# Last 64 query rows of two heads: laid side by side by GpSimd and turned in one transpose

## The chip, the cores and the metric

One core of one Trainium2 chip runs the program. The metric is the time of one execution on the device in microseconds (us), median of several runs. An engine of the core works through its own instructions in order: PE (TensorE matmul; its weight loads are shown apart as PEld), DVE (VectorE), ACT (ScalarE), POOL (GpSimd) and SP (SyncE, which here only issues transfers). Engines wait for each other through semaphores.

## The reference, cut to what matters

Three blocks follow each other on 4 batches of 576 rows by 512 columns: attention with 8 heads of 64 columns, then two feed-forward blocks. The change is in the attention alone.

```python
scores = scale * np.matmul(q, k.transpose(0, 1, 3, 2)) + bias
attn = np.exp(scores - np.max(scores, axis=-1, keepdims=True))
attn = attn / (np.sum(attn, axis=-1, keepdims=True) + 1e-09)
x = np.matmul(attn, v)
x = x.transpose(0, 2, 1, 3).reshape(B, S, H * D)
x = x + relu(layernorm(x) @ w_ch1) @ w_ch2
```

The third block takes x in the same way, with a gate across the rows.

## The kernel before, in words

A first stage (up to some 53 us) works out the bias from the positions, writes it to DRAM and reads it back as tiles. The attention (some 53 to 325 us) follows, then the two feed-forward blocks (to 954 us), where the weights arrive as 64-bit numbers and are converted on DVE, ACT and POOL.

**The attention** goes through 16 units, one for a pair of heads and a batch (`UNITS`). In a unit the 576 query rows of both heads make nine tiles of 128 rows, numbered 0 to 8: four of each head, and tile 4, which holds the last 64 rows of both heads. For a tile PE makes the scores (`S`, line 687), DVE adds the bias and finds the row maximum (`add`, L693), ACT takes the exponent (`exp`, L707), PE turns the result (`T`, L713 and `RT`, L721 and L723), ACT and DVE split it into a high and a low part (`hi`, `lo`). Products with f32 operands are made of such parts, for precision: K, Q and V are split too, by POOL, in `split_k` (L238), `split_q` and `split_v` with the pairs L113 (copy to the high part) and L119 (the rest). `split_k` makes `kh` and `kl` of head 0, then of head 1.

**The outputs.** `PV` (L776) multiplies V with the turned weights, so a head's output comes out turned: 128 partitions (V's high part's 64 columns, then its low part's 64) by 576 rows. `Pev` (L779, ACT) copies each half of 288 rows to the tile `psb` of the head. For the four full tiles `O` (L782) turns 128 columns of `psb` into `OB`; `Oev` copies that to SBUF, `fo` (POOL, L792) adds the two halves of 64, `fx` (POOL, L804) multiplies by the reciprocal of the sum and stores through SP. For the last 64 rows of both heads `Or` (L812) does turning and adding in one: a product of the 64 columns of `psb` with the constant `fold`, two unit matrices of 64 on top of each other. `xr` (DVE, L817) multiplies by the reciprocal and issues two stores from SP.

```python
for h in range(2):
    pe.matmul(PB[64 * h:64 * h + 64, 288:288 + D], lhsT=Psb[h][:, place(4)], rhs=fold, start=True, stop=True)
```

The columns that `place(4)` names are 256 to 319, which lie in both halves of 288, so they are there for both heads after the last of a unit's four `Pev`, called `Pev 1 1`.

**What sets the order.** The table `SEQ` (L27) is the order in which a unit's steps are written out: an entry names a unit relative to the one at hand (`-1` the last one, whose outputs are finished here, `1` the next), a step and its arguments. No scheduler moves anything; each engine gets its instructions in this order. The program of unit u so holds `Pev 1 1`, `Or`, `xr`, `fo`, `fx` of unit u-1, the splits of K and V for unit u+1 (`kh`, `vh`) and of Q for u+2 (`sq`), and the first scores of u+1 (`1 S 0`). At the head of a step `slot` transfers are issued by SP: `slot 0` moves the split Q of the next unit to its place (`place_q`, L236), `slot 5` loads Q and K for u+2 (L210, L216), `vh` loads V. `1 S 0` needs the Q that `place_q` moved and `kh`, `kl` of head 0. The table `END` (L50) is the same for what is left of the last unit, mixed with the layer norms (`N`, `P`), and products (`H`) of the first feed-forward block. In the last units POOL also has the scale of the layer norms (L469 to L473), the applying of some (L479) and splits of the first weights (`w1l`, `w2l`) in its order.

Of the kernel before, what the change touches and what calls it, by code (L numbers as in the profile page):

```python
# [9 lines left out]
F32 = mybir.dt.float32  # L10
# [3 lines left out]
AF = mybir.ActivationFunctionType  # L14
ALU = mybir.AluOpType
# [3 lines left out]
B, H, S, D, DM = 4, 8, 576, 64, 512  # L19
# [8 lines left out]
    0 slot 0, 0 T 0, -1 O 0 1, 0 exp 2, -1 RThi 8 1, -1 lo 8, 0 hi 0, 0 add 3, 0 slot 1, 0 T 1, 0 C 0, -1 RTlo 6 0, 0 add 4, -1 PV 1 0 0 5, -1 RTlo 8 1,  # L28
    0 exp 3, 0 lo 0, 0 S 5, 0 C 1, 0 hi 1, 0 RT 1 0, 0 RThi 1 0, 0 exp 4, -1 O 0 3, 0 lo 1, -1 O 0 2, -1 PV 1 0 5 10, 0 slot 2, 0 T 2, 0 S 6, 0 RTlo 1 0,
    0 add 5, -1 Pev 1 0, 0 hi 2, -1 O 0 0, -1 ra, 0 RT 4 0, 0 slot 3, 0 T 3, -1 PV 1 1 0 1, -1 PV 1 1 1 10, 0 RThi 4 0, 0 lo 2, -1 Oev 0, 0 hi 3, 0 exp 5,  # L30
    0 add 6, 0 RTlo 4 0, 0 kh, -1 Pev 1 1, 0 slot 4, 0 T 4, 0 S 7, 0 hi 4, -1 rb, 0 exp 6, 0 lo 3, 0 S 8, 0 add 7, 0 lo 4, -1 O 1 0, 0 RT 3 1,
    -1 Or, 0 RThi 3 1, -1 O 1 3, -1 O 1 2, 0 PV 0 0 0 2, -1 xr, 0 slot 5, 0 T 5, 0 vh, 0 exp 7, 0 RTlo 3 1, 0 hi 5, 1 S 0, 0 cp, -1 O 1 1, -1 fo 0,
    -1 Oev 1, -1 fo 1, 0 add 8, -1 fx, 0 sq, 0 slot 6, 0 T 6, 0 PV 0 0 2 10, 1 add 0, 0 lo 5, 0 hi 6, 0 exp 8, 0 RT 6 0, 1 S 1, 1 S 2, 0 slot 7, 0 T 7,
    0 RT 8 1, 0 lo 6, 0 Pev 0 0, 1 exp 0, 1 add 1, 0 slot 8, 0 T 8, 0 hi 7, 0 PV 0 1 0 10, 0 RThi 6 0, 0 hi 8, 1 S 3, 1 add 2, 1 S 4, 1 exp 1, 0 Pev 0 1,
# [13 lines left out]
AP_AT = [(15, 0), (15, 1), (15, 4), (15, 5)]  # L48

END = [w.strip() for w in """  # L50
    O 0 1, RThi 8 1, lo 8, RTlo 6 0, PV 1 0 0 5, RTlo 8 1, N 0, N 1, O 0 3, O 0 2, PV 1 0 5 10, Pev 1 0, O 0 0, ra, PV 1 1 0 1, PV 1 1 1 10, N 2, N 3, Oev 0, F 3, Pev 1 1, rb, fo 0, O 1 0, O 1 3, O 1 2, O 1 1, P 0, P 1, H 0 0 6, Or, Oev 1, fo 1, xr, fx, P 2, H 0 6 12, P 3, H 1 0 12
""".split(",")]
WARM = 8
AHEAD = 2
# [45 lines left out]
def block_kernel(  # L100
# [6 lines left out]
    act, dve, pool, pe, sp = nc.scalar, nc.vector, nc.gpsimd, nc.tensor, nc.sync  # L107
# [32 lines left out]
    const = new_pool("const", 1)  # L140
    psT = new_pool("psT", 1, space=PSUM)
    PT = [psT.tile([128, 4, 128], F32, name=f"pt{z}") for z in range(2)]
    ident = const.tile([128, 128], F32, name="ident")
    fold = const.tile([128, 64], F32, name="fold")
    mhalf = const.tile([128, 1], F32, name="mhalf")
    gains = const.tile([128, 8], F32, name="gains")

# [133 lines left out]
    with ExitStack() as c:  # L281
        p = new_pool("bk", 1, c)
# [20 lines left out]
        for f in (load_q, load_k):  # L303
# [9 lines left out]
            out=W.rearrange("p (g h) -> p g h", h=8), in0=w8.unsqueeze(1).to_broadcast([128, 4, 8]), in1=ind.unsqueeze(2).to_broadcast([128, 4, 8]), op=ALU.mult,  # L313
# [98 lines left out]
        for y, z in enumerate(ORDER):  # L412
            mark(f"bias {y}")
            m += [units(n) for n in ORDER[y + AHEAD:][:1]]
            if y in FILL:
                busy(1)
            late.append((z, sums(z, m[y])))
            if y >= BEHIND:
                finish(*late.pop(0))
            if y == WARM_EXP:  # L420
                act.activation(w8[:, :1], mhalf, AF.Exp)
            if y == 5:
                load_v(0, raw0)
# [218 lines left out]
    with ExitStack() as c:  # L642
        smp = new_pool("asm", 1, c)
        sm = smp.tile([128, 48], F32, name="sm")
        SU, RC = [sm[:, 9 * z:9 * z + 9] for z in range(2)], [sm[:, 18 + 9 * z:27 + 9 * z] for z in range(2)]
# [6 lines left out]
        RT = [[atp.tile([128, 2, 320], F32R, name=f"rt{z}{w}") for w in "hl"] for z in range(2)]  # L652
# [3 lines left out]
            dve.memset(t[64:, :, :32].bitcast(F32), 0.0)  # L656
        AT = [tuple(atp.tile([128, 4, S], F32R, name=f"at{h}{w}") for w in "hl") for h in range(2)]
        pp = new_pool("ap", 1, c)
        Psb = [pp.tile([128, S], F32, name=f"psb{h}") for h in range(2)]
        Ob = pp.tile([128, 2, 4, 128], F32, name="ob")  # L660
        xp = new_pool("ax", 1, c)
        M["rc"] = c.enter_context(ExitStack())
        psP = new_pool("psP", 1, c, space=PSUM, side="right")
        PB = psP.tile([128, 512], F32, name="PB")
        OB = psP.tile([128, 512], F32, name="OB")
# [96 lines left out]
        def pv_bank(u, h, x):  # L762
            return SB[0][:, 0] if (u, h, x) == (NU - 1, 1, 1) else PB
# [12 lines left out]
                pe.matmul(d, lhsT=w, rhs=m, start=q == 0, stop=q == len(terms) - 1)  # L776

        def emit_Pev(u, h, x):
            act.activation(Psb[h][:, 288 * x:288 * x + 288], pv_bank(u, h, x)[:, :288], AF.Copy)  # L779

        def emit_O(u, h, t):
            pe.transpose(OB[:, 128 * t:128 * t + 128], Psb[h][:, place(t)], ident)  # L782

        xt = {}

# [22 lines left out]
                M["loads", u]()  # L808

        def emit_Or(u):  # L810
            for h in range(2):
                pe.matmul(PB[64 * h:64 * h + 64, 288:288 + D], lhsT=Psb[h][:, place(4)], rhs=fold, start=True, stop=True)  # L812

        def emit_xr(u):
            hp, b = UNITS[u]
            xr = xp.tile([128, D], F32, name="xr")
            dve.tensor_scalar(out=xr, in0=PB[:, 288:288 + D], scalar1=RC[u % 2][:, 4:5], scalar2=None, op0=ALU.mult)  # L817
            for h in range(2):
                (act if u == NU - 1 else sp).dma_start(out=xs[b][512:, 128 * hp + D * h:128 * hp + D * h + D], in_=xr[64 * h:64 * h + 64])

# [22 lines left out]
        def emit_slot(u, n):  # L843
# [479 lines left out]
def host_arrays(inputs):  # L1323
    q, k, v = (np.asarray(inputs[n]) for n in ("q", "k", "v"))
    d = {}
    qt = q.transpose(0, 1, 3, 2).reshape(B, 4, 2, D, S)
    q2 = np.empty((B, 4, 2, D, S), q.dtype)
    q2[:, :, 0] = qt[:, :, 0]
    q2[:, :, 1, :, :64] = qt[:, :, 1, :, 512:]
    q2[:, :, 1, :, 64:] = qt[:, :, 1, :, :512]  # L1330
    d["q"] = q2.reshape(B, 4, 128, S)
    kt = k.transpose(0, 1, 3, 2).reshape(B, 4, 2, D, S).transpose(0, 1, 3, 2, 4)[:, :, None]
    k2 = np.empty((B, 4, 2, D, 2, S + 64), k.dtype)
    k2[..., :64] = kt[..., 512:]
# [36 lines left out]
    d["moe2_w_sg"] = np.ascontiguousarray(w.transpose(1, 0, 2)).reshape(128, 5 * S)
    return d
# [24 lines left out]
```

## Time and profile before

| | |
|---|---|
| median of 3 runs | 955.36 us (955.33 to 957.57) |
| the profiled execution, its own time | 955.95 us |
| its span, first to last instruction | 954.0 us |
| busy: PE / PEld | 930.1 / 806.4 us |
| busy: DVE / ACT / POOL | 723.2 / 498.2 / 418.5 us |
| granted clock of TensorE, mean | 1.00 (the level of 2.4 GHz) |

A row of the timeline has the start of an instruction, how long it took, the engine, the line, the operation, what it writes and reads, and how many equal ones follow each other. A bracket at the end says how long the engine stood idle before it and what ended that. Where the engine named there had long been done, it was another, often a transfer. Matmuls are pipelined and their ends are modelled, so starts are the better guide on PE and PEld. The first unit's K is split at some 51 us, and a unit takes 16.4 to 17.2 us from then on.

### The profile page before, as it was taken

What the parts mean: (1) busy time and instruction counts of PE and PEld (TensorE: products, weight loads), DVE (VectorE), ACT (ScalarE), POOL (GpSimd) and SP (SyncE); (2) the same over time, 40 slices, a digit from 0 to 9 for tenths busy, and PEclk for the clock granted to TensorE, in tenths of its full rate; (3) what the DMA queues carried; (4) which work ended last, traced back from release to release, by engine and by line L of the source; (5) the groups of instructions that cost most, each with busy time, mean ns of one, the idle gap of its engine ahead of it and who ended that gap; (6) DMA issues with size and microseconds to landing.
All of it is one profiled execution on the core that took longest, in us unless ns stands there. A gap on an engine that the chain in (4) does not pass through costs nothing. (4 is left out here: it accounts for less than half of the span.)

```text
span 954.0 us, 16102 instructions
## 1 busy us (share of the span) xinstructions
PE 930.1 (97%) x5729; PEld 806.4 (85%) x5729; DVE 723.2 (76%) x1441; ACT 498.2 (52%) x1108; POOL 418.5 (44%) x523
## 2 busy tenths in 40 slices
PE   7889999999999999999999999999999999999997
PEld 2269999999999778888888888888788998989996
DVE  7988999999889587886679797979755656455452
ACT  8979999999998654221222222322132635253340
POOL 0057787878888634332223343334300523143241
PEclk9999999999999999999999999999999999999999
DMA  6878766748643451103032323332321100001001
GB/s 237 278 232 258 217 186 197 224 133 265 193 140 109 158 189 45 67 21 110 21 98 98 119 90 122 98 110 84 120 71 67 59 1 12 34 1 56 1 35 66
DMA packets 58127, 110.26 MB, mean 116 GB/s; under 512 B 10176, under 2 KB 21184, under 8 KB 57792
## 3 DMA queue, kind: packets, MB, share of 16 engines
q1 hardware_dynamic: 56960, 108.38, 35.5%
q8 instruction: 45, 0.74, 0.3%
q10 hardware_dynamic: 1088, 0.87, 0.3%
q14 instruction: 34, 0.28, 0.1%
HBM read 71.41 MB, written 28.38 MB: 105 GB/s over the span
## 5 line engine op out<-in xcount | busy, mean ns | idle before, releaser
L123 PE MATMUL psh<-blk,w1h 128*128 128x512 f32 (+1 forms) x640 | 151.5, 368 | 1.1 <-DVE blk L119 1.0
L176 POOL TENSOR_TENSOR cvl<-cvl,cvt 128x512 f32<-128x512 f32 x44 | 56.9, 1293 | 207.8 <-DVE cvt L173 188.3
L638 ACT ACTIVATE hh<-psh 128x512 fp32r<-128x512 f32 (+1 forms) x80 | 43.8, 553 | 179.3 <-PE psh L123 179.1
L123 PEld LDWEIGHTS psh<-blk,w1h 128*128 128x128 f32 x640 | 113.3, 188 | 22.2 <-PE OB L782 1.2
L693 DVE CUSTOM_DVE_ANT_0 ct<-s,bias 128x576 f32<-128x576 f32 x144 | 107.1, 752 | 17.5 <-PE s L687 9.8
L707 ACT ACTIVATE a<-ct,sm 128x576 f32<-128x576 f32 x144 | 112.1, 779 | 3.5 <-DVE sm L693 2.9
L1043 DVE TENSOR_TENSOR x_sb<-psy,x_sb 128x512 f32<-128x512 f32 x144 | 97.3, 683 | 9.1 <-PE psy L123 8.6
L639 DVE SCALAR_TENSOR_TENSOR hl<-psh,hh 128x512 fp32r<-128x512 f32 (+1 forms) x80 | 50.5, 633 | 56.2 <-ACT hh L638 56.2
L123 PE MATMUL psy<-w2h,hh 128*128 128x512 f32 x288 | 90.9, 396 | 1.3 <-ACT hh L638 0.7
L123 PE MATMUL psy<-w2l,hh 128*128 128x512 f32 x288 | 88.9, 390 | 0.0
L123 PE MATMUL psy<-w2h,hl 128*128 128x512 f32 x288 | 88.8, 390 | 0.0
L713 PE MATMUL pt<-ident,a 128*128 128x128 f32 x576 | 85.1, 273 | 0.7 <-DVE at0l L119 0.7
L123 PE MATMUL psh<-blk,w1l 128*128 128x512 f32 (+1 forms) x320 | 79.0, 368 | 0.0
L687 PE MATMUL s<-kh,q 128*128 128x288 f32 x320 | 72.0, 314 | 3.2 <-DVE sm L693 1.8
L713 PEld LDWEIGHTS pt<-ident,a 128*128 128x128 f32 x576 | 68.6, 140 | 2.0 <-DVE at0l L119 1.4
L687 PE MATMUL s<-kl,q 128*128 128x288 f32 x320 | 65.9, 295 | 0.0
L123 PEld LDWEIGHTS psh<-blk,w1l 128*128 128x128 f32 x320 | 56.8, 188 | 10.0
L123 PEld LDWEIGHTS psy<-w2h,hl 128*128 128x128 f32 x288 | 54.1, 188 | 11.5
L123 PEld LDWEIGHTS psy<-w2l,hh 128*128 128x128 f32 x288 | 54.0, 188 | 11.4
L123 PEld LDWEIGHTS psy<-w2h,hh 128*128 128x128 f32 x288 | 52.3, 188 | 12.8 <-DVE x_sb L1043 2.0
L177 POOL TENSOR_TENSOR cvw<-cvl,cvw 128x512 f32<-128x512 f32 x44 | 60.0, 1364 | 3.5
L687 PEld LDWEIGHTS s<-kh,q 128*128 128x128 f32 x320 | 48.9, 189 | 5.8 <-DVE sm L693 2.7
(191 smaller groups left out, 2171.5 us busy)
## 6 DMA issues: line engine op xcount, KB each, us to landing
r<-in_moe_w_ch_dram SPq DMA_DIRECT2D x32, 512.0 KB, 4.9
k<-in_k_dram SPq DMA_DIRECT2D x16, 640.0 KB, 4.7
q<-q SPq DMA_DIRECT2D x64, 144.0 KB, 3.9
scr<-o SPq DMA_DIRECT2D x24, 295.5 KB, 3.2
v<-in_v_dram SPq DMA_DIRECT2D x16, 384.0 KB, 5.5
q<-in_q_dram SPq DMA_DIRECT2D x16, 288.0 KB, 3.0
bias<-scr SPq DMA_DIRECT2D x8, 576.0 KB, 5.9
bias<-scr SPq DMA_DIRECT2D x8, 512.0 KB, 6.5
```

What stands on the lines that cost most here:

```text
L123: pe.matmul(ps, lhsT=w, rhs=x, start=start and j == 0, stop=stop and j == len(terms) - 1)
L176: pool.tensor_tensor(out=T["l"], in0=T["l"], in1=T["t"].bitcast(F32), op=ALU.mult)
L177: pool.tensor_tensor(out=T["w"], in0=T["l"], in1=T["w"], op=ALU.add)
L638: act.activation(hh[:, f, :n], ps[:, :n], AF.Relu)
L639: dve.scalar_tensor_tensor(out=hl[:, f, :n], in0=ps[:, :n], scalar=0.0, in1=hh[:, f, :n].bitcast(F32), op0=ALU.max, op1=ALU.subtract)
L687: pe.matmul(s[:, x, :288], lhsT=w, rhs=m[:, 288 * x:288 * x + 288], start=j == 0, stop=j == len(prs) - 1)
L693: dve.tensor_tensor_reduce(out=ct, in0=s[:, :, :288], in1=bias[UNITS[u][0]][:, n].rearrange("p (a b) -> p a b", a=2), scale=-0.125, scalar ...
L707: act.activation(weights(n), ct.rearrange("p a b -> p (a b)"), AF.Exp, scale=-1.0, bias=mt, accum_out=SU[u % 2][:, n:n + 1])
L713: pe.transpose(PA[k % 2][:, j], e[:, 128 * j:128 * j + 128], ident)
L1043: dve.tensor_tensor(out=x_sb[:, t], in0=ps, in1=x_sb[:, t], op=ALU.add)
```

## The change

`Psb` becomes one tile for both heads. A new step `oc` has POOL copy the last 64 rows of both heads side by side into the new tile `Pr` (128 by 2 by 64). `Or` turns `Pr` in one transpose against the unit matrix instead of two products with `fold`, which goes with its load. `xr` scales 128 columns instead of 64 on DVE, and POOL adds the two halves of 64 before the two stores. In `SEQ` the step `Pev 1 1` with `oc` behind it now stands ahead of `kh`, where `kh` stood first; in `END` `oc` stands behind `Pev 1 1`.

```diff
-    0 add 6, 0 RTlo 4 0, 0 kh, -1 Pev 1 1, 0 slot 4, 0 T 4, ...
+    0 add 6, 0 RTlo 4 0, -1 Pev 1 1, -1 oc, 0 kh, 0 slot 4, 0 T 4, ...
...
-    ... Oev 0, F 3, Pev 1 1, rb, fo 0, ...
+    ... Oev 0, F 3, Pev 1 1, oc, rb, fo 0, ...
...
-        Psb = [pp.tile([128, S], F32, name=f"psb{h}") for h in range(2)]
+        Psb = pp.tile([128, 2, S], F32, name="psb")
+
+        Pr = pp.tile([128, 2, 64], F32, name="pr")
...
         def emit_Or(u):
-            for h in range(2):
-                pe.matmul(PB[64 * h:64 * h + 64, 288:288 + D], lhsT=Psb[h][:, place(4)], rhs=fold, start=True, stop=True)
+            pe.transpose(PB[:, 288:416], Pr.rearrange("p h c -> p (h c)"), ident)
+
+        def emit_oc(u):
+            pool_copy(Pr, Psb[:, :, place(4)])
...
+            w = xp.tile([128, 2 * D], F32, name="xw")
             xr = xp.tile([128, D], F32, name="xr")
-            dve.tensor_scalar(out=xr, in0=PB[:, 288:288 + D], scalar1=RC[u % 2][:, 4:5], scalar2=None, op0=ALU.mult)
+            dve.tensor_scalar(out=w, in0=PB[:, 288:416], scalar1=RC[u % 2][:, 4:5], scalar2=None, op0=ALU.mult)
+            pool.tensor_tensor(out=xr, in0=w[:, :D], in1=w[:, D:], op=ALU.add)
```

How this moves instructions is read from the order of the two programs (line numbers of the changed one are one or two lower). First POOL's order in one unit, before: `sm` is a step for the reciprocal, `kh` and `kl` are K's splits for the next unit, `v` those of V, `x<-ob` the step `fo`.

```order
L795 TENSOR_SCALAR sm<-sm 128x9 [waits Activation_49]
L113 TENSOR_SCALAR kh<-k 128x640 [waits DMAHW5_49,PE_49]
L119 TENSOR_TENSOR kl<-k,kh 128x640 [waits PE_49,Pool_49]
L113 TENSOR_SCALAR kh<-k 128x640
L119 TENSOR_TENSOR kl<-k,kh 128x640 [waits Pool_49]
L113 TENSOR_SCALAR v_103<-v 128x12x64 [waits DMAHW6_49,PE_49]
L119 TENSOR_TENSOR v_103<-v,v_103 128x12x64 [waits Pool_49]
L792 TENSOR_TENSOR x<-ob 128x4x64 [waits DMAHW0_49,Activation_49]
```

The same piece of the changed program:

```order
L794 TENSOR_SCALAR sm<-sm 128x9 [waits Activation_49]
L113 TENSOR_SCALAR pr<-psb 128x128 [waits Activation_49]
L113 TENSOR_SCALAR kh<-k 128x640 [waits DMAHW4_49]
L119 TENSOR_TENSOR kl<-k,kh 128x640 [waits Pool_49]
L113 TENSOR_SCALAR kh<-k 128x640
L119 TENSOR_TENSOR kl<-k,kh 128x640 [waits Pool_49]
L820 TENSOR_TENSOR xr<-xw 128x64 [waits DMAHW2_49,DMAHW1_49,DVE_49]
L113 TENSOR_SCALAR v_102<-v 128x12x64 [waits DMAHW5_49,PE_49]
L119 TENSOR_TENSOR v_102<-v,v_102 128x12x64 [waits Pool_49]
L791 TENSOR_TENSOR x<-ob 128x4x64 [waits DMAHW7_49]
```

The copy, which waits for `Pev 1 1` on ACT, now stands ahead of both heads' `kh` and `kl`, and the addition `xr<-xw` ahead of V's split.

On PE the steps from `Or` to `1 S 0` stood so before (`s<-kh` and `s<-kl` in the last rows are the next unit's first scores):

```order
L782 MATMUL OB<-ident,psb_891 128x128 [waits Activation_49]
L723 MATMUL s_905<-ident,a_866 128x128
L812 MATMUL PB<-fold,psb_890 64x64 [waits Activation_49]
L812 MATMUL PB<-fold,psb_891 64x64
L782 MATMUL OB<-ident,psb_891 128x128 x2
L776 MATMUL PB<-at0h,v_104 128x288 [waits Activation_49,Pool_49]
L776 MATMUL PB<-at0h,v_104 128x288
L713 MATMUL pt_73<-ident,a_865 128x128 [waits DVE_49]
L713 MATMUL pt_73<-ident,a_865 128x128 x3
L687 MATMUL s_901<-kh,q_101 128x288 [waits DMAHW2_49,DMAHW3_49,DVE_49,Pool_49]
L687 MATMUL s_901<-kh,q_101 128x288
L687 MATMUL s_901<-kl,q_101 128x288 [waits Pool_49]
```

And now:

```order
L781 MATMUL OB<-ident,psb 128x128 [waits Activation_49]
L722 MATMUL s_903<-ident,a_864 128x128
L810 MATMUL PB<-ident,pr 128x128 [waits Pool_49]
L781 MATMUL OB<-ident,psb 128x128 x2
L775 MATMUL PB<-at0h,v_103 128x288 [waits Activation_49]
L775 MATMUL PB<-at0h,v_103 128x288
L712 MATMUL pt_73<-ident,a_863 128x128 [waits DVE_49]
L712 MATMUL pt_73<-ident,a_863 128x128 x3
L686 MATMUL s_899<-kh,q_100 128x288 [waits DMAHW1_49,DMAHW2_49,DVE_49,Pool_49]
L686 MATMUL s_899<-kh,q_100 128x288
L686 MATMUL s_899<-kl,q_100 128x288 [waits Pool_49]
```

One transpose stands where two products stood and waits for POOL instead of ACT; the order on PE is the same otherwise. The wait of `s<-kl` for POOL was there before; it is for `kl` of head 0.

The last piece is POOL's in the last unit's program, of the changed kernel (`t<-t,rs` applies a layer norm, `w2l` is a weight's low part, `pr` the copy):

```order
L476 TENSOR_SCALAR t<-t,rs 128x512 [waits DMAHW4_49]
L794 TENSOR_SCALAR sm<-sm 128x9 [waits Activation_49]
L563 TENSOR_SCALAR gains<-gains 128x4
L119 TENSOR_TENSOR w2l<-t,w2h 128x512
L113 TENSOR_SCALAR pr<-psb 128x128 [waits Activation_49]
L119 TENSOR_TENSOR w2l<-t,w2h 128x512
L820 TENSOR_TENSOR xr<-xw 128x64 [waits DMAHW4_49,DMAHW3_49,DVE_49]
```

Before, nothing of `Or` hung on this order; now the copy comes behind the first `w2l`.

## Rows read from the trace of the kernel before

**Rows 1.** The page's first part: busy us (share of the span) xinstructions.

```profile
PE 930.1 (97%) x5729; PEld 806.4 (85%) x5729; DVE 723.2 (76%) x1441; ACT 498.2 (52%) x1108; POOL 418.5 (44%) x523
```

**Rows 2.** Windows: us, PE, PEld, DVE, ACT, POOL busy, clock, DMA share, GB/s.

```profile
62.00:67.00 5.00, 3.12 (x22) 2.48 (x22) 3.73 (x12) 3.52 (x11) 2.61 (x2) 1.00 1.00 321
...
255.00:272.00 17.00, 17.00 (x140) 16.77 (x140) 14.10 (x39) 15.52 (x42) 13.25 (x16) 1.00 0.71 224
```

**Rows 3.** Timeline of PEld (weight loads) in unit 12's program: start, us, what.

```profile
262.70 0.14 PEld L782 LDWEIGHTS OB<-ident,psb 128*128 128x128 f32 x1
262.83 0.14 PEld L723 LDWEIGHTS s<-ident,a 128*128 128x128 f32 x1
...
263.40 0.20 PEld L782 LDWEIGHTS OB<-ident,psb 128*128 128x128 f32 x2
...
264.53 0.33 PEld L687 LDWEIGHTS s<-kl,q 128*128 128x128 f32 x2
```

**Rows 4.** Timeline of ACT: the step Pev 1 1 in units 9, 12, 13 and 14.

```profile
212.95 0.41 ACT L779 ACTIVATE psb<-PB 128x288 f32<-128x288 f32 x1
...
261.83 0.40 ACT L779 ACTIVATE psb<-PB 128x288 f32<-128x288 f32 x1
...
278.21 0.40 ACT L779 ACTIVATE psb<-PB 128x288 f32<-128x288 f32 x1
...
294.58 0.40 ACT L779 ACTIVATE psb<-PB 128x288 f32<-128x288 f32 x1
```

**Rows 5.** Timeline of PEld: 1 S 0 in unit 9.

```profile
215.41 0.33 PEld L687 LDWEIGHTS s<-kl,q 128*128 128x128 f32 x2
```

**Rows 6.** Timeline of POOL in units 12 to 15.

```profile
255.69 0.73 POOL L113 TENSOR_SCALAR kh<-k 128x640 fp32r<-128x640 f32 x1
256.50 1.58 POOL L119 TENSOR_TENSOR kl<-k,kh 128x640 fp32r<-128x640 f32 x1
...
261.59 0.83 POOL L113 TENSOR_SCALAR v<-v 128x768 fp32r<-128x768 f32 x1 [1.16 <-PE PB L776]
...
273.46 0.73 POOL L113 TENSOR_SCALAR kh<-k 128x640 fp32r<-128x640 f32 x1
...
283.05 1.20 POOL L804 TENSOR_TENSOR x<-x,sm 128x256 f32<-128x256 f32 x2
...
289.53 0.73 POOL L113 TENSOR_SCALAR kh<-k 128x640 fp32r<-128x640 f32 x1
...
310.96 2.53 POOL L119 TENSOR_TENSOR w2l<-t,w2h 128x512 fp32r<-128x512 f32 x2
```

**Rows 7.** Groups of POOL by form: xcount | busy us, mean ns of one | idle before.

```profile
L119 POOL TENSOR_TENSOR grl<-sq,grh 128x64 fp32r<-128x64 f32 x16 | 5.2, 327 | 0.0
L113 POOL TENSOR_SCALAR x2h<-rh 128x256 fp32r<-128x256 f32 x4 | 1.6, 410 | 33.8 <-ACT rh L116 33.8
L113 POOL TENSOR_SCALAR w<-m 128x1 f32<-128x1 f32 x1 | 0.2, 192 | 45.5 <-DVE m L335 45.5
```

**Rows 8.** Timeline of SP: loads for the layer norms, then place_q for unit 15.

```profile
288.89 1.75 SPq L610 DMA_DIRECT2D t<-xs  x4
290.75 2.41 SPq L236 DMA_DIRECT2D q<-q  x4
```

**Rows 9.** Timeline of PEld: 1 S 0 of unit 15, and Or in unit 15's program.

```profile
297.26 0.30 PEld L687 LDWEIGHTS s<-kh,q 128*128 128x128 f32 x2 [0.20 <-POOL v L119]
...
313.11 0.20 PEld L812 LDWEIGHTS PB<-fold,psb 128*64 128x64 f32 x4 [0.17 <-issue]
```

**Rows 10.** The tile q: issue to landing of its transfers.

```profile
DMA to landing us min/median/max: 2.4/3.5/7.8
```

**Rows 11.** Timeline of POOL and of PE at the end of the attention.

```profile
329.09 1.43 POOL L792 TENSOR_TENSOR x<-ob 128x256 f32<-128x256 f32 x2
...
328.09 0.34 PE L812 MATMUL PB<-fold,psb 128*64 128x64 f32 x4
```

More of the change, by code (lines that the diff above doesn't have):

```diff
@@ L30 @@
     0 add 5, -1 Pev 1 0, 0 hi 2, -1 O 0 0, -1 ra, 0 RT 4 0, 0 slot 3, 0 T 3, -1 PV 1 1 0 1, -1 PV 1 1 1 10, 0 RThi 4 0, 0 lo 2, -1 Oev 0, 0 hi 3, 0 exp 5,
-    0 add 6, 0 RTlo 4 0, 0 kh, -1 Pev 1 1, 0 slot 4, 0 T 4, 0 S 7, 0 hi 4, -1 rb, 0 exp 6, 0 lo 3, 0 S 8, 0 add 7, 0 lo 4, -1 O 1 0, 0 RT 3 1,
+    0 add 6, 0 RTlo 4 0, -1 Pev 1 1, -1 oc, 0 kh, 0 slot 4, 0 T 4, 0 S 7, 0 hi 4, -1 rb, 0 exp 6, 0 lo 3, 0 S 8, 0 add 7, 0 lo 4, -1 O 1 0, 0 RT 3 1,
     -1 Or, 0 RThi 3 1, -1 O 1 3, -1 O 1 2, 0 PV 0 0 0 2, -1 xr, 0 slot 5, 0 T 5, 0 vh, 0 exp 7, 0 RTlo 3 1, 0 hi 5, 1 S 0, 0 cp, -1 O 1 1, -1 fo 0,
@@ L50 @@
 END = [w.strip() for w in """
-    O 0 1, RThi 8 1, lo 8, RTlo 6 0, PV 1 0 0 5, RTlo 8 1, N 0, N 1, O 0 3, O 0 2, PV 1 0 5 10, Pev 1 0, O 0 0, ra, PV 1 1 0 1, PV 1 1 1 10, N 2, N 3, Oev 0, F 3, Pev 1 1, rb, fo 0, O 1 0, O 1 3, O 1 2, O 1 1, P 0, P 1, H 0 0 6, Or, Oev 1, fo 1, xr, fx, P 2, H 0 6 12, P 3, H 1 0 12
+    O 0 1, RThi 8 1, lo 8, RTlo 6 0, PV 1 0 0 5, RTlo 8 1, N 0, N 1, O 0 3, O 0 2, PV 1 0 5 10, Pev 1 0, O 0 0, ra, PV 1 1 0 1, PV 1 1 1 10, N 2, N 3, Oev 0, F 3, Pev 1 1, oc, rb, fo 0, O 1 0, O 1 3, O 1 2, O 1 1, P 0, P 1, H 0 0 6, Or, Oev 1, fo 1, xr, fx, P 2, H 0 6 12, P 3, H 1 0 12
 """.split(",")]
@@ L143, in block_kernel @@
     ident = const.tile([128, 128], F32, name="ident")
-    fold = const.tile([128, 64], F32, name="fold")
     mhalf = const.tile([128, 1], F32, name="mhalf")
@@ L427, in block_kernel @@
                 sp.dma_start(out=ident, in_=a["c_ident"])
-            if y == 10:
-                sp.dma_start(out=fold, in_=a["c_fold"])
             if y == QK[0]:
@@ L778, in emit_Pev @@
         def emit_Pev(u, h, x):
-            act.activation(Psb[h][:, 288 * x:288 * x + 288], pv_bank(u, h, x)[:, :288], AF.Copy)
+            act.activation(Psb[:, h, 288 * x:288 * x + 288], pv_bank(u, h, x)[:, :288], AF.Copy)
         def emit_O(u, h, t):
-            pe.transpose(OB[:, 128 * t:128 * t + 128], Psb[h][:, place(t)], ident)
+            pe.transpose(OB[:, 128 * t:128 * t + 128], Psb[:, h, place(t)], ident)
         xt = {}
@@ L865, in block_kernel @@
             slot=emit_slot, sq=emit_sq, kh=emit_kh, vh=emit_vh, C=emit_C, cp=lambda u: emit_C(u, 2), S=emit_S, add=emit_add, exp=emit_exp, T=emit_T, hi=emit_hi, lo=emit_lo, RT=emit_RT, RThi=emit_RThi,
-            RTlo=emit_RTlo, PV=emit_PV, Pev=emit_Pev, O=emit_O, Oev=emit_Oev, fo=emit_fo, fx=emit_fx, Or=emit_Or, ra=emit_ra, rb=emit_rb, xr=emit_xr,
+            RTlo=emit_RTlo, PV=emit_PV, Pev=emit_Pev, O=emit_O, Oev=emit_Oev, fo=emit_fo, fx=emit_fx, Or=emit_Or, oc=emit_oc, ra=emit_ra, rb=emit_rb, xr=emit_xr,
         )
@@ L1356, in host_arrays @@
     d["c_log"] = np.log1p(pos).reshape(1, S)
-    d["c_fold"] = np.concatenate([np.eye(D), np.eye(D)]).astype(np.float32)
     d["c_ident"] = np.eye(128, dtype=np.float32)
```

## The prediction

> **What bounds the kernel now.** I read the page first: PE is busy in 97% of the span, no other engine in more than 76% [rows 1]. A mean over stages is not enough, so I went to the windows, one of about a unit of the attention: PE is busy in 17.00 us of 17.00, its weight loads in 16.77, DVE in 14.10, ACT in 15.52, POOL in 13.25 [rows 2]. So in the attention PE sets the time: what is taken off PE there is gained, what makes PE wait there is lost, and the other engines matter only by when they let PE go on. Then I read the timeline around `Or`, and last the order of POOL's instructions in both programs, since the change moves work there.
>
> **Part 1, the cheaper `Or`.** The weight load of the transpose ahead of `Or` starts at 262.83, that of the transpose behind it at 263.40 [rows 3]: 0.57 us. Between two transposes without `Or` the step is 0.13 (262.70 to 262.83) [rows 3], so the two products cost 0.57 - 0.13 = 0.44. A transpose in their place costs 0.13. PE saves 0.31 a unit, 16 x 0.31 = 5.0 us, if nothing else changes.
>
> **Part 2, what it waits for.** The copy needs `Pev 1 1`, and in `SEQ` it now stands ahead of `kh` and `kl`. POOL works in order, so K's split for the next unit can't begin before `Pev 1 1` has ended. Before, POOL did it far ahead: in unit 12 `kh` began at 255.69, `Pev 1 1` ended at 262.23 [rows 4, 6]. The one who waits is `1 S 0` on PE, whose second pair of products reads `kl` of head 0; all of PE's later work queues behind it. In unit 12 its weight load came at 264.53 [rows 3], 2.30 us after the end of `Pev 1 1`. That is the gap into which POOL must now fit:
>
> - hand-over from ACT: 0.08, as between `kh` and `kl` (255.69 + 0.73 to 256.50) [rows 6];
> - the copy, 128 elements a partition: no row shows it. The same operation takes 0.19 for 1 element and 0.41 for 256 [rows 7]; it lies half way, I take 0.30;
> - hand-over 0.08, `kh` with its hand-over 0.81, `kl` 1.58 [rows 6].
>
> Sum 2.85 us against a gap of 2.30, so `kl` is 0.55 late. It is late by the clock of `Pev 1 1`, not of `Or`, so the 0.31 saved at `Or` is only waited away: PE stands for 0.86 and nets a loss of 0.55. This happens in the 14 units' programs that have both an earlier unit to finish and a next one to split: 14 x 0.55 = 7.7 us. Bounds: with the copy at 0.19 or 0.41 the loss is 0.44 or 0.66 a unit. The smallest gap is unit 9's, 212.95 + 0.41 to 215.41 = 2.05 [rows 4, 5], a loss of 0.80, with the long copy 0.91. On the other side ACT might run `Pev 1 1` sooner once PE is late: V's split, which waits for the same last product, began at 261.59, so at most 261.83 - 261.59 = 0.24 sooner [rows 4, 6]; then the loss is 0.31, with the short copy 0.20. So 2.8 to 12.7 us.
>
> **Part 3, POOL's whole chain is late.** Everything behind the copy on POOL moves: both heads' splits, the new addition, V's split, `fo`, `fx`, Q's split. In unit 13 POOL ran without a pause from `kh` at 273.46 to the end of `fx` at 284.25, 10.79 us [rows 6]. Now it starts at 278.61 (end of `Pev 1 1`) [rows 4] + 0.46 for copy and hand-overs, has the addition more (128 by 64, 0.33 as the like one [rows 7], and 0.08), and ends at 290.3, 6.0 later. On SP the two `xr` stores wait for POOL's addition instead of DVE, the loads of Q, K and V behind them; then `fx`'s store. In most units this has room: Q's split ends some 13 us after `Pev 1 1` (the 11.7 of unit 13, and Q's own split), `place_q`'s transfers land 3.5 later (2.4 to 7.8) [rows 10], and `1 S 0` wants them about 19 after it (a unit and the gap). In the four units in which POOL also converts weights the room is gone; I put 1.0 for them together, 0 to 3.
>
> It has no room in unit 14. There SP loads what unit 12's `fx` stored, at 288.89, and only then issues `place_q` for unit 15, at 290.75 [rows 8]. The scores that need it started at 297.26 after a wait of 0.20, put down to V's split, which they don't need; of what they do need only these transfers could be late [rows 9]. Six us later is 303.3; PE would come there at 297.26 + 2 x 0.55 = 298.4. So 4.9 us, of which I take 4.5, since transfers that start later may meet less traffic. The second place is `Or` in unit 15's program: from 289.53 to the end of the first `w2l`, 312.2 [rows 6], POOL has 21 us of work without its pauses; started at 294.98 + 0.46 [rows 4], with the addition and the copy, it lets `Or` go at 317.4 instead of 313.1 + 0.55 [rows 9]. That is 3.7, and is covered when PE has already lost 4.5 in unit 14. The two are one term: 4.5, from 0 to 4.9.
>
> **Part 4, the end.** In `END` the copy stands behind the last layer norm scales on POOL, which end at 329.09; `Or` stood at 328.09 [rows 11]. It now comes at 329.4. PE may lose 1.4; the last `fx`, for which ACT waits there, is later by copy and addition, 0.7. I take 0.9.
>
> **What costs nothing.** DVE's `xr` on twice the columns and the dropped load of `fold`: DVE has 3 us a unit to spare [rows 2], and the load stands in the first stage. Were DVE full, it would be 64 columns more a unit, under 0.1 us.
>
> **The sum.** 7.7 + 1.0 + 4.5 + 0.9 = 14.1 us on the profiled execution's own time, 955.95 (span 954.0), which is 0.6 above the median shown. So 970.0 on that one, **969.4** as a median.
>
> **Rivals.**
>
> *The wait fits.* If `kl` were ready when PE asks, the 0.31 of `Or` would be gained in every unit: 955.4 - 5.0 = **950.4**, faster. It decides at a gap of 2.85 + 0.31 after the end of `Pev 1 1`. For it speaks that ACT's step may come sooner; against it, that at most 0.24 is to be had there [rows 4, 6], where 0.55 is needed to break even, and that `kh` and `kl` alone take 2.39 of a gap of 2.30. 6%. That both effects cancel, near 955, gets 3%.
>
> *Only the short wait.* ACT runs `Pev 1 1` as soon as it can and transfers land early: 14 x 0.25 + 0.9 + 2 for part 3 = 6.4, **962**. For it speaks that ACT has spare time as soon as PE waits; against it that ACT was at 15.5 of 17 [rows 2]. 14%.
>
> *Late Q in more units.* If `place_q`'s transfers take 7.8 instead of 3.5 [rows 10], Q lands at 21 against 19, 2 us late. In the four or five units with most traffic that is 8 to 10 us more: **978**. Against it, the long landings are the rare ones. 7%.
>
> *A slower TensorE after the waits.* Granted clock is 1.00, the level of 2.4 GHz, even where PE was busy for only 3.12 of 5 us [rows 2]; no row shows the other level, 1.2. A fall would add half of PE's time for as long as it lasted: from a stop at 298 to the end at 325 at most 13 us; I put 5, **974**. 3%. The Trainium skill ("TensorE: Matmul & The Clock Gate", "HAM oscillation — how this bites in real kernels") says that PE left idle for long between products falls to half clock and must be busy again to come back; by that rule the stop of 4.5 us in unit 14 is the one that could do it. The pauses before the attention in this trace did not, but they were shorter.
>
> *That the transpose saves nothing* would not show: in 14 units the saving is waited away.
>
> **Numbers.** The forecast has 67%, its own range 964 to 975. The range of 8 in 10 takes in the milder case and most of part 2's upper bound: 961 to 976; outside lie the faster cases and the late Q. A measurement of this kernel can tell 0.3%, 2.9 us, from no change: faster by more than that 0.06, within it 0.03, slower 0.91.
>
> **What would show it.** In the profile after: PE's `kl` products of `1 S 0` with an idle time of 0.7 to 1.0 before them, put down to POOL's `kl`, in 14 units (some 12 us in all); `kh` on POOL starting right behind the copy, 0.4 after `Pev 1 1`; the copy near 0.30; a unit's period near 16.9 instead of 16.4; one stop of PE of 3 to 5 us between units 14 and 15, ended by a transfer of Q or by the copy; `Or` at 0.13. The rest of the kernel, from 336 on, only shifted. I am wrong if `kl`'s products don't wait, or if the units keep their period.

## The result, and the profile after

The changed kernel takes 967.37 us in the median of five runs (966.18 to 968.89), beside 955.81 us for the kernel before (955.33 to 961.0, five runs): ratio 1.0121, 95% interval 1.0101 to 1.0141. It is 11.6 us slower. The profiled execution took 968.89 us, its span is 967.1 us.

The busy times of the page, first part, show nothing of this loss (the row that answers to [rows 1]):

```profile
PE 932.9 (96%) x5681; PEld 809.5 (84%) x5681; DVE 727.2 (75%) x1441; ACT 496.0 (51%) x1108; POOL 426.5 (44%) x555
```

The list of waits of PEld in the attention (74 to 340 us) does: line, what it waited for, us in total, times, longest.

```profile
PEld s L686 <- POOL kl L119: 8.8, 12, 1.0
PEld s L686 <- POOL xr L820: 4.3, 1, 4.3
...
PEld s L686 <- issue: 0.9, 1, 0.9
```

In the kernel before, `kl` stands nowhere in this list. One unit shows how the wait comes about. ACT's `Pev 1 1`, then POOL, then PEld (timeline: start, us, what; the idle time before it in brackets), in unit 12's program, which answers to [rows 3, 4, 6]:

```profile
269.49 0.40 ACT L778 ACTIVATE psb<-PB 128x288 f32<-128x288 f32 x1
```

```profile
269.97 0.30 POOL L113 TENSOR_SCALAR pr<-psb 128x128 f32<-128x128 f32 x1 [1.20 <-ACT psb L778]
270.23 0.73 POOL L113 TENSOR_SCALAR kh<-k 128x640 fp32r<-128x640 f32 x1
271.04 1.56 POOL L119 TENSOR_TENSOR kl<-k,kh 128x640 fp32r<-128x640 f32 x1
272.57 0.73 POOL L113 TENSOR_SCALAR kh<-k 128x640 fp32r<-128x640 f32 x1
273.38 1.57 POOL L119 TENSOR_TENSOR kl<-k,kh 128x640 fp32r<-128x640 f32 x1
274.92 0.32 POOL L820 TENSOR_TENSOR xr<-xw 128x64 f32<-128x64 f32 x1
```

```profile
270.48 0.14 PEld L722 LDWEIGHTS s<-ident,a 128*128 128x128 f32 x1
270.59 0.14 PEld L810 LDWEIGHTS PB<-ident,pr 128*128 128x128 f32 x1
270.70 0.25 PEld L781 LDWEIGHTS OB<-ident,psb 128*128 128x128 f32 x2
...
272.66 0.30 PEld L686 LDWEIGHTS s<-kl,q 128*128 128x128 f32 x2 [0.73 <-POOL kl L119]
```

`Or` itself is as cheap as hoped: its weight load is 0.11 us behind the one ahead of it and 0.11 ahead of the next. But POOL idles 1.20 us until `Pev 1 1` is done, and only then copies and splits K; PE's `kl` products wait 0.73 us for that.

The one long stop is in unit 14's program. PEld and SP there:

```profile
304.77 0.49 PEld L712 LDWEIGHTS pt<-ident,a 128*128 128x128 f32 x4
309.54 0.30 PEld L686 LDWEIGHTS s<-kh,q 128*128 128x128 f32 x2 [4.28 <-POOL xr L820]
```

```profile
300.24 1.75 SPq L607 DMA_DIRECT2D t<-xs  x4
302.09 2.91 SPq L235 DMA_DIRECT2D q<-q  x4
```

The bracket names POOL's `xr`, but that had ended at 308.79 and these products do not read it. What they need is the Q that SP sends from 302.09 on, 11 us later than before [rows 8]. For PE's products behind these loads the view of the tile `q` (296 to 312 us) names that transfer (us, times):

```profile
  DMA q<-q: 4.1, 1
```

Behind the stop the granted clock falls (windows: busy time of PE, PEld, DVE, ACT and POOL, then the clock, DMA share and GB/s):

```profile
306.00:308.00 2.00, 0.00 (x0) 0.00 (x0) 1.87 (x5) 0.18 (x1) 1.92 (x3) 1.00 0.75 144
308.00:310.00 2.00, 0.42 (x3) 0.46 (x4) 0.10 (x2) 0.00 (x0) 1.92 (x4) 0.96 0.20 64
310.00:312.00 2.00, 2.00 (x11) 1.97 (x11) 1.32 (x3) 0.85 (x2) 1.83 (x3) 0.50 0.07 14
312.00:314.00 2.00, 2.00 (x12) 1.95 (x11) 0.74 (x2) 1.47 (x5) 1.68 (x6) 0.69 0.00 0
314.00:316.00 2.00, 2.00 (x19) 2.00 (x18) 1.48 (x5) 1.61 (x6) 1.99 (x4) 1.00 0.00 0
```

To place the rest I took the start of every unit's `Or` on PE from the traces. The table has the first of the 16, the mean period of the next 13, the period with the stop, the last period, and the time from the last `Or` to the end of the span. The kernels below the first two are those of the experiments.

| kernel | first `Or` | mean of 13 periods | unit 13 to 14 | unit 14 to 15 | from there to the end |
|---|---|---|---|---|---|
| before | 82.11 | 16.44 | 17.22 | 14.98 | 625.9 |
| changed | 84.75 | 16.89 | 22.14 | 16.11 | 624.5 |
| 1: only the wait | 83.74 | 16.90 | 18.92 | 17.30 | 625.2 |
| 2: K split first | 85.76 | 16.81 | 18.41 | 16.16 | 622.4 |
| 3: K split first in unit 13 | 82.47 | 17.04 | 21.33 | 17.59 | 625.0 |
| 4: K split first, sum behind `fx` | 84.92 | 16.05 | 16.99 | 16.13 | 627.2 |
| 5: changed order, sum behind `fx` | 82.95 | 16.93 | 21.29 | 16.16 | 628.3 |
| 6: K split first, sum by DVE | 82.32 | 16.76 | 18.20 | 16.11 | 624.0 |
| 7: same, a half from PSUM | 82.26 | 16.34 | 17.23 | 16.14 | 623.8 |

The 13.1 us between the two spans so are: 2.64 before the first `Or`, 13 x 0.445 = 5.8 in the units, 4.92 at the stop, 1.13 in the last unit, and 1.4 less behind it. The 2.64 is not the change's: kernels 3 and 5, with the same order and the same work up to there, reach that place at 82.47 and 82.95. Of the 2.64, 1.52 are there when the first unit's scores begin, first in the kernel before, then in the changed one:

```profile
52.86 0.53 PE L687 MATMUL s<-kh,q 128*128 128x288 f32 x2 [0.86 <-ACT o L354]
```

```profile
54.38 0.53 PE L686 MATMUL s<-kh,q 128*128 128x288 f32 x2 [0.86 <-ACT o L353]
```

In the first stage of the changed kernel's profiled execution the clock had fallen (0.72 from 14 to 20 us, where it was 1.00 in the kernel before); whether that alone makes the 1.52 is not shown. The other 1.1 come in the first unit, where the clock fell again (0.64 from 68 to 72 us, 1.00 in the kernel before). That leaves 10.5 us for the change in the profiled executions, within the interval of the medians (9.7 to 13.5).

### The profile page after: what moved, and what is told of

It is laid out like the page before. It is cut to its first block, busy times and chain, and to the rows that moved or that the text cites. A ratio compares the mean times of both kernels' runs of the same rounds, so it can differ in the third digit from the quotient of the medians.

```text
span 967.1 us, 15962 instructions
## 1 busy us (share of the span) xinstructions
PE 932.9 (96%) x5681; PEld 809.5 (84%) x5681; DVE 727.2 (75%) x1441; ACT 496.0 (51%) x1108; POOL 426.5 (44%) x555
```

## The experiments

My theory was that the place of the copy on POOL makes the loss: K's split waits for `Pev 1 1`. The rival was that the new operations cost it: transpose, copy, or sum. Dots in a diff stand for what is left out. Medians and ratios are against the kernel before on the same chip in the same series; its medians there were 956.1 to 957.0 us.

**1. Only the wait.** The kernel before, with its product and DVE's `xr` (but `psb` as one tile), and only the copy added, at its new place. Nothing reads the copy.

```diff
-    ... 0 kh, -1 Pev 1 1, ...
+    ... -1 Pev 1 1, -1 oc, 0 kh, ...
...
+        def emit_oc(u):
+            pool_copy(Pr, Psb[:, :, place(4)])
```

> The kernel before, with its product with fold and VectorE's multiplication, to which only the copy oc is added, at the place that the change gives it (Pev 1 1, oc, kh); nothing reads the copy. Theory (the wait alone makes the loss): every unit is later by 0.4 to 0.5 us at the kl products, 0.31 us more a unit at the product than in the changed kernel if that stands on the path, and a stop of 2 to 5 us comes between units 14 and 15: 966 us (962 to 970). Rival (the transpose or GpSimd's sum make the loss): 955.5 to 958 us.

Measured: 967.04 us, ratio 1.0117 (1.0095 to 1.0138), a loss as large as the change's, without its transpose and its sum. The waits of PEld in the attention:

```profile
PEld s L689 <- POOL kl L119: 5.8, 12, 0.7
...
PEld s L689 <- POOL kh L113: 2.3, 1, 2.3
```

The rival falls. The units take 16.90 us, as with the transpose (16.89), but `kl` makes PE wait less, 5.8 us against 8.8 in 12 units: 0.25 a unit. That is about the saving of `Or`, and it shows that in the changed kernel it is only waited away. The expectation had added the product's 0.31 to the unit if it stood on the path; it does not. That the totals agree so well is in part chance: the stop costs less here than in the changed kernel (1.70 beside 4.92), where Q's transfers took longer (median 6.5 us to landing, 5.3 here), and the last unit more. It is 2.3 longer than before: PE's `psh` products wait 2.51 us ahead of `Or` (1.20 before). As before they start 0.11 us after DVE has made the low part of `blk`; that is late here (337.28 to 337.94), behind layer norm statistics that had waited 1.12 us for their load.

**2. K split first.** The changed kernel whole, with the old order put back.

```diff
-    ... -1 Pev 1 1, -1 oc, 0 kh, ...
+    ... 0 kh, -1 Pev 1 1, -1 oc, ...
```

> The changed kernel whole, with GpSimd's order put back: kh and kl of the next unit stand ahead of Pev 1 1 and the copy oc, as they did before. Theory (the loss is the wait of kh and kl behind the copy): the products with kl stop for nothing any more, the stop between units 14 and 15 goes or shrinks to under 2 us, and the transpose's 0.31 us a unit shows: 951 us (949 to 956), against 955.8 before the change and 967.4 with it. Rival (the transpose, the copy or the sum by GpSimd are slow in themselves): 964 us or more.

Measured: 963.33 us, ratio 1.0070 (1.0051 to 1.0089). Neither: my 951 is far off. `kl` has left the waits of PEld, but something took its place:

```profile
PEld PB L810 <- POOL pr L113: 10.3, 8, 1.7
PEld pt L712 <- DVE at0l L119: 3.2, 6, 0.8
```

POOL's timeline over one unit says why:

```profile
253.68 0.29 POOL L113 TENSOR_SCALAR pr<-psb 128x128 f32<-128x128 f32 x1
255.44 0.32 POOL L820 TENSOR_TENSOR xr<-xw 128x64 f32<-128x64 f32 x1 [1.46 <-DVE xw L819]
255.72 0.84 POOL L113 TENSOR_SCALAR v<-v 128x768 fp32r<-128x768 f32 x1
...
266.18 0.73 POOL L113 TENSOR_SCALAR kh<-k 128x640 fp32r<-128x640 f32 x1
...
269.34 1.57 POOL L119 TENSOR_TENSOR kl<-k,kh 128x640 fp32r<-128x640 f32 x1
270.87 0.30 POOL L113 TENSOR_SCALAR pr<-psb 128x128 f32<-128x128 f32 x1
```

From one copy to the next it is 17.19 us, and the 1.46 before the sum is all of POOL's idle time in them. POOL copies, waits for PE to turn and DVE to scale, adds, and has some 15 us of other work (here 2.6 of it a conversion of weights) before it comes to the next copy, for which `Or` waits. It is a ring that runs through three engines and leaves POOL no slack here. In 8 of the 16 units `Or` waits for the copy; in seven of the others POOL still comes early and waits 0.9 to 2.3 us for `Pev 1 1`. In the changed kernel the sum is not waited for, because K's split stands between copy and sum. So the change has two places at which POOL can hold up PE, and the order hides one of them at a time.

**3. K split first in one unit.** Only unit 13's program has the old order.

```diff
+            early = u in (13,)
+                if early and name == "kh":
+                    continue
+                if early and w == "-1 Pev 1 1":
+                    emit["kh"](u)
```

> The changed kernel; in the program of unit 13 alone kh stands ahead of Pev 1 1 and oc, so that GpSimd's K split of unit 14, and all that follows it there, is no longer late. Theory (stop of unit 14 and late Q are one term with the copy's lateness; Or of unit 15 then waits instead): TensorE stops 2 to 4 us at another place, 966 us (965 to 967.5). Rival (the stop goes with its cause in one unit): 0.45 us of the kl wait and 4.3 us of the stop go, and with them the 1.3 us of the clock's fall: 961 to 963 us.

Measured: 970.99 us, ratio 1.0150 (1.0129 to 1.0171), above both expectations and slower than the changed kernel by the medians. The rival (961 to 963) falls. As the theory has it, the wait moves to `Or`:

```profile
PEld PB L810 <- POOL pr L113: 6.1, 2, 3.6
```

The 3.6 is in unit 15's program, whose copy POOL makes at 324.95, behind the low parts of the first weights; in the changed kernel it ends at 326.03, with `Or` at 326.45. So the stop in unit 14 covers a second limit, and without it at most 0.4 us was to be had there as long as POOL's work stays. The other 2.5 is `Or` in unit 13's program, where K's split, late as ever, now stands ahead of the copy; with the last unit (17.59) this makes the kernel slower than expected. One unit out of step loses more than it gains.

**4. The sum behind `fx`.** As 2, with POOL's sum and its stores as a step of its own.

```diff
-    ... -1 fx, 0 sq, ...
+    ... -1 fx, -1 xa, 0 sq, ...
...
+        def emit_xa(u):
...
+            pool.tensor_tensor(out=xr, in0=w[:, :D], in1=w[:, D:], op=ALU.add)
```

> As the first of these runs (kh ahead of Pev 1 1 and oc), and GpSimd's sum of the halves with its two stores split off into a step of its own behind fx, so that VectorE's product, not the sum, is all that xr issues there; then no GpSimd instruction of the next unit stands behind the wait for Or. Theory: the K split and the V split of the next unit are never late: 950.5 us (948.5 to 953), up to 1 us under the first run. Rival (the sum's place does not matter, or its stores come late): the same as the first run within 0.5 us, or 1 to 2 us over it.

Measured: 953.99 us, ratio 0.9979 (0.9966 to 0.9991); 9 us less than 2, where I had expected one at most. The ring is open:

```profile
260.83 0.30 POOL L113 TENSOR_SCALAR pr<-psb 128x128 f32<-128x128 f32 x1 [0.29 <-ACT psb L778]
261.09 0.85 POOL L113 TENSOR_SCALAR v<-v 128x768 fp32r<-128x768 f32 x1
...
266.35 0.33 POOL L825 TENSOR_TENSOR xr<-xw 128x64 f32<-128x64 f32 x1
```

Most units take 16.03 us, 0.34 less than the 16.37 of the kernel before: here the cheaper `Or` is gained, at the 0.31 of the prediction's first part.

**5. The sum behind `fx`, in the changed order.** As 4, with the two steps in the changed order; it fills the table of two by two.

```diff
-    ... 0 kh, -1 Pev 1 1, -1 oc, ...
+    ... -1 Pev 1 1, -1 oc, 0 kh, ...
```

> The changed kernel with its order (Pev 1 1, oc, kh), and only the sum and its stores behind fx. Together with the three other kernels this fills a table of two by two: K split first or not, sum late or not. Theory (in the changed order the copy's wait has already made GpSimd late enough that the sum waits for nothing, and the loss is the wait of the K split alone): 967 us (965 to 970), units of 16.8 us, kl products waiting 0.7 to 1.0 us as in the changed kernel. Rival (the sum behind Or is a loss of its own, as it is with the K split first, where moving it gave 9 us): 958 to 961 us.

Measured: 970.18 us, ratio 1.0144 (1.0127 to 1.0160), just above the range that I expected. Here the sum's place gains nothing, as the theory has it. PE's `kl` products wait 10.1 us in 12 units. The stop is there too, and the clock falls behind it:

```profile
307.14 0.30 PEld L686 LDWEIGHTS s<-kh,q 128*128 128x128 f32 x2 [3.11 <-issue]
```

```profile
308.00:310.00 2.00, 2.00 (x11) 1.95 (x10) 1.62 (x4) 1.48 (x3) 1.91 (x2) 0.50 0.00 0
```

| us, median | sum right behind `Or` | sum behind `fx` |
|---|---|---|
| copy, then K's split | 967.37 | 970.18 |
| K's split, then copy | 963.33 | 953.99 |

**6. The sum by DVE.** As 2, but DVE makes the sum, so that POOL waits for nothing behind the copy.

```diff
-            pool.tensor_tensor(out=xr, in0=w[:, :D], in1=w[:, D:], op=ALU.add)
+            dve.tensor_tensor(out=xr, in0=w[:, :D], in1=w[:, D:], op=ALU.add)
```

> As the run with the K split first (sum in xr, right behind VectorE's product), but VectorE makes the sum, not GpSimd. Theory (with the K split first the loss left over is a ring: copy, transpose, VectorE's product, GpSimd's sum, and behind it GpSimd's whole work up to the next copy, 15.5 us of work and 1.35 us of waiting a unit): the ring is open, TensorE waits for pr in no unit but the last, units of 16.0 to 16.1 us, 954.5 us (952 to 957). Rival (the copy is late because the K split stands ahead of it, whoever makes the sum): 961 to 965 us.

Measured: 959.97 us, ratio 1.0037 (1.0024 to 1.0050). 3.4 us come back, not nine, which lies between what the theory and the rival gave. `pr` is gone from PEld's waits but for two, and results of DVE stand there:

```profile
PEld pt L712 <- DVE at0l L119: 4.5, 8, 1.2
PEld s L722 <- DVE sm L692: 2.8, 6, 1.0
PEld PB L810 <- POOL pr L113: 2.7, 2, 1.7
```

DVE and POOL at one such place:

```profile
268.61 0.34 DVE L819 TENSOR_SCALAR xw<-PB,sm 128x128 f32<-128x128 f32 x1
268.99 1.18 DVE L820 TENSOR_TENSOR xr<-xw 128x64 f32<-128x64 f32 x1
270.08 0.28 DVE L119 TENSOR_TENSOR rt0l<-s,rt0h 128x128 fp32r<-128x128 f32 x1
```

```profile
268.25 1.84 POOL L119 TENSOR_TENSOR v<-v,v 128x768 fp32r<-128x768 f32 x1
270.04 1.43 POOL L791 TENSOR_TENSOR x<-ob 128x256 f32<-128x256 f32 x2
```

The sum of 64 elements a partition takes 1.18 us and ends at 270.17, 0.08 after POOL's `v` (270.09). In 14 of the other 15 units it also ends 0.07 or 0.08 after an instruction of POOL (in 12 of them the same one), however early it began; in the one left it took 0.22. The next row of DVE handles twice the elements in 0.28.

**7. DVE's sum with a half in PSUM.** As 6, but the second half alone is scaled into SBUF, and one instruction scales the first half from PSUM and adds.

```diff
-            dve.tensor_tensor(out=xr, in0=w[:, :D], in1=w[:, D:], op=ALU.add)
...
+            dve.scalar_tensor_tensor(out=xr, in0=PB[:, 288:288 + D], scalar=RC[u % 2][:, 4:5], in1=w[:, D:], op0=ALU.mult, op1=ALU.add)
```

> As the run in which VectorE makes the sum, but of a half in PSUM and a half in SBUF (a product of the second half into SBUF, then product and sum in one instruction), where that run's sum had both halves in SBUF and took 0.75 us in the median, 0.22 to 1.50, ending when GpSimd's instruction beside it ended. Theory (an instruction of VectorE with both inputs in SBUF waits for GpSimd's to end, one with an input in PSUM does not): 0.3 us each, units of 16.0 to 16.1 us, 954.5 us (953 to 956.5). Rival (VectorE is simply late there and the sum's length is chance): 0.6 us or more each, 958 to 961 us.

Measured: 952.44 us, ratio 0.9960 (0.9947 to 0.9973). The sums, from the answer for their line in 6 and in 7 (ns least, median, most):

```profile
L820 DVE TENSOR_TENSOR xr<-xw x16: 224/749/1501, 83.5 to 335.3; 128x64 f32<-128x64 f32 x16
```

```profile
L820 DVE SCALAR_TENSOR_TENSOR xr<-PB,sm,xw x16: 283/284/285, 83.4 to 328.7; 128x64 f32<-128x64 f32 x16
```

With one input in PSUM none of the 16 is held up, and the kernel is 7.5 us faster, a little below the range that I expected: the theory stands. Not all units reach 16.03 (mean 16.34); POOL waits for late loads of Q in seven of them, 9.1 us in all, which was not part of any theory.

**8. No copy by POOL at all.** As 4, but ACT writes `pr` straight from PSUM. The kernel lays columns 512 to 575 there instead of 256 to 319, and leaves them out of `psb`, where old values stay: other rows are turned, with the same work, and only the time is of use.

```diff
+            n = 224 if x else 288
-            act.activation(Psb[:, h, 288 * x:288 * x + 288], pv_bank(u, h, x)[:, :288], AF.Copy)
+            act.activation(Psb[:, h, 288 * x:288 * x + n], pv_bank(u, h, x)[:, :n], AF.Copy)
+            if x:
+                act.activation(Pr[:, h, :], pv_bank(u, h, x)[:, n:288], AF.Copy)
```

> As the run with the sum behind fx, but without GpSimd's copy: ScalarE writes the last 64 rows of each head straight from PSUM into pr (224 and 64 elements in two instructions, for 288 in one). GpSimd then waits for Pev in no unit. Theory (the copy, put behind the K split, costs nothing any more): the same as that run, 954 us (952 to 956), with units of 16.0 us. Rival (the copy still holds up GpSimd or the transpose): 950 to 952 us; or, if ScalarE's extra 0.2 to 0.5 us a unit stand on the path, 957 to 962 us.

Measured: 954.95 us, ratio 0.9985 (0.9972 to 0.9997), as 4. Behind K's split the copy on POOL costs nothing more in the units (mean of 13 periods 16.12, in 4 16.05).

**9 to 12. Towards the fastest version.** 9 is 4 with the last unit's copy by ACT, 10 is 4 with all copies by ACT, 11 is 7 with the last unit's copy by ACT, 12 is 9 with the last unit's sum ahead of `fx`. The edit of 9 and 11, then that of 10, then that of 12:

```diff
         def emit_oc(u):
-            pool_copy(Pr, Psb[:, :, place(4)])
+            if u == NU - 1:
+                act.activation(Pr, Psb[:, :, place(4)], AF.Copy)
+            else:
+                pool_copy(Pr, Psb[:, :, place(4)])
```

```diff
-            pool_copy(Pr, Psb[:, :, place(4)])
+            act.activation(Pr, Psb[:, :, place(4)], AF.Copy)
```

```diff
-    ... xr, fx, xa, P 2, ...
+    ... xr, xa, fx, P 2, ...
```

> As the run with the K split first and the sum behind fx; in the last unit alone ScalarE, not GpSimd, makes the copy into pr, so that the transpose there does not wait behind GpSimd's work for the next layer (1.7 us in that run's trace). Theory: the wait goes, 952.5 us (951 to 954). Rival (what follows the last unit waits for something else): 954 us, as that run.

> As the run with the K split first and the sum behind fx, with every copy into pr made by ScalarE instead of GpSimd (0.25 to 0.3 us a unit more on ScalarE). Theory (GpSimd's copy behind the K split is hidden, but for the last unit's 1.7 us): 952.5 us (951 to 954.5), units of 16.03 us. Rival (ScalarE's extra 0.3 us a unit stand on the path): 956 to 959 us.

> The two edits that helped, together: K split first, VectorE's sum of a half in PSUM and a half in SBUF, and the last unit's copy by ScalarE. Theory (the last unit's wait for pr, 1.7 us in the run with VectorE's sum from PSUM, goes and nothing takes its place): 951 us (950 to 953), 0.994 to 0.995 of the kernel before. Rival (the end of the last unit waits for something else): 952.4 us, as without it.

> As the run with the last unit's copy by ScalarE, but in the last unit the sum of the halves and its stores stand ahead of fx again. From the last Or to the end of the span the four kernels of these runs that had the sum behind fx there took 626.7 to 628.6 us, those with it ahead of fx 622.4 to 625.4. Theory (the late stores of the last unit hold up the loads and layer norms that follow): 625.5 us or less from the last Or to the end, 951.5 us in the median (950 to 953). Rival (that difference comes from elsewhere): 627 us or more, 953.5 us.

Measured: 953.49 (0.9966, 0.9955 to 0.9978), 954.36 (0.9974, 0.9962 to 0.9986), 953.29 (0.9966, 0.9952 to 0.9981) and 953.90 us (0.9962, 0.9948 to 0.9977). In 9, 11 and 12 the last period falls from 16.1 to 14.7 us, so the wait for `pr` there is gone. Of the 1.5 us the median shows little, and 11 and 12 came out above the ranges that I expected: the intervals of 4, 7 and 9 to 12 overlap, and I can't rank them. 12 takes 627.4 us from its last `Or` to the end, so the theory on the late stores falls; why that part differs from 622 to 628 us between kernels stays open. All six are faster than the kernel before, by 0.2 to 0.4%.

## Why the prediction was right

**The time.** Forecast 969.4 (961 to 976, slower with 0.91); measured 967.37. The likeliest case came, with its mechanism.

**Part 1** holds: 0.31 a unit forecast; 0.34 is gained where nothing waits (experiment 4), and it is only waited away in the changed kernel (experiment 1).

**Part 2, 7.7 us, was somewhat too large.** From the end of `Pev 1 1` (269.89) to the weight load of the `kl` products (272.66) it is 2.77 us, where I summed 2.85. The copy took exactly the 0.30 that I had put half way between two sizes, but `kh` began 0.04 before the copy's recorded end, where I had a hand-over of 0.08. So 0.445 a unit in place of 0.55, and 13 periods carry it: 5.8. In one of them a pause that the kernel before has anyway (17.11 us from unit 4 to 5, where the changed kernel takes 16.88) takes up part of the lateness. The products wait 0.73, in 12 units, not in 14.

**Part 3.** The 1.0 for the units in which POOL converts weights is hardly there: one wait of 0.9, in the 5.8 above. The stop of unit 14 is at its place, 4.28 us long, for the transfers forecast; its period is 4.92 longer, beside 4.5. That the sizes are so near is in part luck. The transfers were sent 11.3 us later than before, where PE came 8.2 later (305.26, before 297.06), so POOL's chain gave 3.1 and not 4.9; most of the rest came from slower transfers (median 6.5 us to landing, 5.7 before), where I had hoped for less traffic. That it and unit 15's `Or` are one term was borne out by experiment 3: with the stop gone, `Or` waits 3.6 us for the copy.

**Part 4.** 0.9 forecast; PE waits 1.27 us for the copy in the last unit, where I had up to 1.4, and the unit loses 1.13, but what follows is 1.4 shorter, in a part that varies by as much between kernels. It can't be told from zero.

**The sum** of 14.1 compares with 11.6 in medians. The over-estimate is part 2 and the weight units: 8.7 forecast, 5.8 measured. The terms as measured add up to 10.5; no row shows what the medians have beyond that, which is less than their interval.

**The rivals.** "The wait fits" needed K's split 0.55 earlier; it was 0.08 earlier. "A slower TensorE after the waits" came true beside the forecast, not in place of it: 0.50 and 0.69 of the clock for 2 us each. I had 5 us for it; the two rows cost about 2 x 0.50 + 2 x 0.31 = 1.6, and POOL's copy, for which unit 15's `Or` would have waited until 326.03 in any case, hides all but about 0.4 of that. The rule from the Trainium skill ("TensorE: Matmul & The Clock Gate", "HAM oscillation — how this bites in real kernels"), that PE left idle for long falls to half clock, agrees with these rows. Why the clock fell in the first stage and the first unit as well, where PE stood for at most 2.2 us at a time, no run shows.

**What I did not see:** the second wait, POOL's sum behind `Or` and DVE. I had costed the addition at its 0.33 us and a hand-over. The order of the change hides it, so the forecast did not suffer; but experiment 2, which I expected at 951, came out 12 us higher for it.

## What to carry to other kernels

A short helper put on an in-order engine must be costed by what queues behind it: here 0.30 us of copy moved 10 us of POOL's work behind an event of ACT. Look for the ring as well: an engine that hands something to another and, before its other work, waits for it back has no slack left once its own work nearly fills the unit. With K's split first, putting the consumer where its input has long been ready was worth 9 us. Putting the producer behind work that doesn't depend on it gave 4 us alone and left the kernel slower than before; both together made it faster.

## What the runs showed of the hardware

**DVE held up by POOL.** An instruction of DVE with both inputs in SBUF took 0.75 us in the median and up to 1.50 for 64 elements, ending 0.08 after POOL's instruction beside it; with one input in PSUM it took 0.284 each time. The Trainium skill ("SBUF — State Buffer", "Who interferes with whom") says that such an instruction shares a read port with GpSimd and is blocked until GpSimd's has ended, and that with at most one input in SBUF, outside modes that use both ports, it is not; experiments 6 and 7 agree.

**The clock after a stop.** After stops of 4.28 us (changed kernel), 3.64 us (experiment 3) and 3.11 us (experiment 5) the next 2 us of work had a granted clock of 0.50, the lower of the two levels (1.2 GHz); after 2.31 us (experiment 1) it stayed at 1.00, from 304 to 324 us. The stop's length alone does not settle it: after the 2.51 us at the end of the attention in experiment 1 the clock fell too. Experiment 3, then experiment 1:

```profile
325.00:327.00 2.00, 1.69 (x8) 1.68 (x9) 0.89 (x4) 0.87 (x2) 1.50 (x2) 0.50 0.00 0
```

```profile
340.00:342.00 2.00, 2.00 (x9) 1.53 (x6) 0.28 (x1) 0.00 (x0) 2.00 (x5) 0.50 1.04 377
```

In the first unit of the changed kernel it fell to 0.50 as well, in a stretch with no stop above 1.2 us but with PE half idle:

```profile
66.00:68.00 2.00, 1.04 (x7) 0.86 (x8) 1.05 (x6) 1.24 (x5) 0.18 (x1) 0.88 1.02 387
68.00:70.00 2.00, 2.00 (x10) 1.98 (x11) 1.91 (x5) 0.63 (x4) 0.00 (x0) 0.50 1.03 395
```

That happened in 7 of the 14 profiled executions. In them it is 30.4 to 31.3 us from the first unit's first scores to the first `Or`, in the other seven 29.2 to 30.2. It is not the kernel that decides: 9 and 12 differ in the last unit alone, and the clock stayed in 9 and fell in 12. What sets it is open. With the 1.5 us that were late before the first unit, the profile of the changed kernel carries 2.6 us that are no part of the change.
